# Ten mixing groups on one core: the step that follows each group is taken at a higher rate, and the first scores of the next attention are ordered differently

## The chip, the cores and the metric

The kernel runs on one core of one Trainium2 chip. The metric is the device time of one execution in microseconds, and lower is better. The core has a matrix engine (TensorE, PE in the rows; its weight loads are PEld), a vector engine (VectorE, DVE), an activation engine (ScalarE, ACT), GpSimd (POOL), and SyncE (SP), which issues nearly all transfers of this kernel, in its own order.

## The reference

Three layers follow each other on 8 batches of 576 tokens, 512 wide (8 heads of 64).

```
p_packed = sm_attn(p, k, v)              # 32 packed rows per head look at the 576 tokens
out      = sm_attn(q, p_packed, p_packed)# 576 tokens look at the 32 packed rows
x        = heads put side by side
u        = x + real(fft2(x))             # over tokens and channels of a batch
ch       = relu(norm(u) @ w_ch1) @ w_ch2 # 512 -> 2048 -> 512
y        = u + ch
logits   = y @ w_gate                    # 8 experts; a second gate decides per token whether
e        = argmax or the expert before   # it takes its own expert or that of the token before
out      = p[e] * (relu(y @ w1[e]) @ w2[e])
```

## The kernel before

Nearly every product is made of three fp16 products of high and low halves (`PASS`, line 162), so TensorE does most of the work and the other engines split, evict and normalize.

**Stages.** The attention and the transform of batch 0 come first. Then ten groups of the channel layer follow, in the order 0, 1, 2, R0, 3, 4, 5, 6, R1, 7 (line 1146). A numbered group is a batch's 512 tokens; R0 and R1 hold the 256 tokens of four batches that don't fill a tile. Behind them the experts' blocks run (`e1`, `e2`).

**A group** (`Mix`) has 16 first products `mm1(f)` (12 matmuls each, written `hp`) and 16 second products `mm2(f)` (12 matmuls each, 6 for R0 and R1, written `acc`), two steps apart. The last two second products of a group run between the first two first products of the next one. A numbered group so has 384 matmuls of its own.

**Beside it** run generators, which `tick` advances: the attention of the next batch at `ATT_RATE`, the splitting of the experts' weights at `EW_RATE`, and `after_mix` of the group before at `LAST_RATE`. A numbered group gives 2 ticks a step f, 28 from f = 2 to 15; R0 and R1 give 14. `after_mix` has four tiles (two for R0 and R1). For each it scales the tile into high and low halves (`xh`), transposes them by a transfer into the one buffer `xt`, stores them to `XS`, and later makes eight small matmuls `lp` (the logits) that VectorE evicts (`lsum`). It takes some 23 advances for four tiles. What isn't done when the next group begins is then taken at once (`drain`).

**Attention's steps around the change**, in their order: first scores (`scores`, line 361; per half of the heads, two tiles of 4 matmuls, written `s1`), their greatest, the exponentials, halves and a transposing transfer (`turn`: `ehl` to `et`), the product with v (`pps`, for which v is loaded and split, `vhl`), its transposition (`ptp`), and the second scores (`s2`, from q, loaded and split as `qh`, and `pth`). Then come the transform's products over channels (`gp`) and over tokens (`bp`, `zd`, `P`, `Q`, `X`).

**Buffers.** Attention and logits share two PSUM buffers (`psA`, tag `att`). k, v and q share two buffers (tag `qkv`): a half of v is loaded when the first scores have read that half of k, and a half of q when v is split.

**Order.** A scheduler takes the ready instruction of the smallest number, where numbers follow the program. `tc.high_priority(offset=SOON)` lowers an instruction's number by 200, so it may stand earlier than the code says. Each engine, SyncE too, then runs its own list in order. `scores` takes a PSUM buffer with its first matmul there.

Of the kernel before, what the change touches and what calls it, by code (L numbers as in the profile page):

```python
# [164 lines left out]
EW_RATE = 1.3  # L165
EWS = 2
CW0, CW1 = 5, 2
LAST_RATE = 1.2
R0_RATE = 1.6
R1_RATE = 1.2  # L170
AHEAD = 3
SOON = 200
# [7 lines left out]
def _build(tc, nc, ctx, A, stop):  # L180
# [132 lines left out]
    def attention(b):  # L313
        count = [0]

        def att(nm):
            count[0] += 1
            if b == 0 and count[0] % 3:
                return psO.tile([128, 512], F32, tag="o", name=nm)
            return psA.tile([128, 512], F32, tag="att", name=nm)  # L320
# [26 lines left out]
        pt = ap.tile([128, 4, 32], F32, tag="pt", name=f"p{b}")  # L347
# [3 lines left out]
        kts, vts, q32, qts = [], [], [], []  # L351
# [7 lines left out]
        s1, mxs, e32s = {}, {}, {}  # L359

        def scores(hf):
            s1[hf] = [att(f"s1_{b}_{hf}_{i}") for i in range(2)]

            for i in range(2):
                for p2 in range(2):
                    for r in range(2):
                        d, row = slice(64 * r, 64 * r + 64), 64 * p2 + 32 * r
                        nc.tensor.matmul(s1[hf][i][row:row + 32, :288], pt[d, 2 * hf + p2],  # L368
                                         kts[hf][d, p2, 288 * i:288 * i + 288], start=True, stop=True)
            (load_v if b else load_q)(hf)  # L370

        def greatest(hf):
# [21 lines left out]
        for steps in (((scores, 0),), ((greatest, 0),), ((exps, 0), (scores, 1)), ((turn, 0), (greatest, 1)),  # L394
                      ((exps, 1),), ((turn, 1),)):
            for fn, hf in steps:
                with tc.high_priority(offset=SOON if fn in (scores, greatest, exps) else 0):
                    fn(hf)
            yield
        rs = ap.tile([128, 2], F32, tag="rs", name=f"rs{b}")  # L400
# [8 lines left out]
        for hf in range(2):  # L409
# [13 lines left out]
            n = 0  # L423
# [133 lines left out]
        for k, (cs, hf) in enumerate(((0, 0), (0, 1), (1, 0), (1, 1))):  # L557
# [3 lines left out]
            for i in range(2):  # L561
                for n, (x, y) in enumerate(PASS):
                    nc.tensor.matmul(bp[:, :w], aeo[i][:, x, cs, cols], cst[:, 4 * i + 2 * cs + y, :w],  # L563
                                     start=i + n == 0, stop=False)
# [7 lines left out]
            if k == 2:  # L572

                zd = att(f"zd{b}")
                n = 0
# [460 lines left out]
    for n, _ in enumerate(attention(0)):  # L1036
        if n == CW0:
            while wdone[0] < CW1:
                next(cw)
            nc.sync.dma_start(cdt, A["cdt"])  # L1040
            nc.sync.dma_start(c3, A["c3"])
            nc.sync.dma_start(cst, A["cst"])
        if n == 30:
            wgf = wp.tile([128, 4, 9], F32, name="wgf")
            nc.sync.dma_start(wgf, A["wg"])
            nc.sync.dma_start(c16, A["c16"])
            nc.sync.dma_start(i32r, A["i32r"])
            nc.sync.dma_start(i32v, A["i32v"])
            nc.sync.dma_start(c32, A["c32"])
            split(wgh[:, :, 0], wgh[:, :, 1], wgf, 64.0)  # L1050
# [95 lines left out]
    for b in [0, 1, 2, "R0", 3, 4, 5, 6, "R1", 7]:  # L1146
# [11 lines left out]
        if prev is not None:  # L1158
            if last is not None:
                drain(last)  # L1160
            last = after_mix(prev.tiles)
            bg.append([last, 0.0, LAST_RATE])
        if not isinstance(b, str):
            if b + 1 < NB:
                ga = attention(b + 1)
                bg.append([ga, 0.0, ATT_RATE])
            if b == 1:
                bg.append([ew, 0.0, EW_RATE])
            if b == 7:
                actx.close()  # L1170
                open_moe()
                drain(ew)
                drain(last)
                r0 = routing(0)
                bg.append([r0, 0.0, R0_RATE])
# [69 lines left out]
```

## Time and profile before

| | |
|---|---|
| median of 3 runs (lowest, highest) | 1516.62 us (1511.03, 1521.59) |
| profiled execution, its own time | 1514.66 us |
| span in its trace | 1512.9 us |
| granted TensorE clock, mean | 0.971 |
| TensorE busy | 1403.3 us (93% of the span) |
| VectorE busy | 769.0 us (51%) |
| ScalarE busy | 460.5 us (30%) |

The page's busy times count instructions, not progress: the end of a matmul is modelled. Its slices show TensorE at nine tenths or more from the second tenth of the span on, and the granted clock at full speed nearly throughout. A row of the waits names the engine and line that waited and whom for; the time is idle time of that engine just before the instruction.

### The profile page before, as it was taken

To read this page: it belongs to the slowest core of one execution; us is meant where nothing else is said; L and a number is where in the kernel's file an instruction comes from. 1 tells how busy PE (TensorE), PEld (TensorE's weight loads), DVE (VectorE), ACT (ScalarE), POOL (GpSimd) and SP (SyncE) were. 2 spreads that over 40 slices of the span, in tenths; PEclk is the share of its full clock that TensorE was granted. 3 is DMA by queue.
4 is the path that set the end of the run, shared out by engine and by line. 5 is a ranking of instruction groups with operands and counts; after the bars stand their busy time and mean duration, and the time that the engine had idled before them with its cause. 6 is when DMAs were issued, how large, how long until landed. Compare 5 with 4: busy or idle time off the path is not lost. (4 is left out here: it accounts for less than half of the span.)

```text
span 1512.9 us, 28826 instructions
## 1 busy us (share of the span) xinstructions
PE 1403.3 (93%) x11340; PEld 825.5 (55%) x11340; DVE 769.0 (51%) x1615; ACT 460.5 (30%) x858; POOL 278.9 (18%) x296
## 2 busy tenths in 40 slices
PE   4588888998999899999999999999899999999996
PEld 3334434544564454454444456455677677777764
DVE  5789977567655766666766665433531111111110
ACT  3343444344333434434435333111111111111111
POOL 1312113203200420320321220000212121121211
PEclk6689999999999999999999999999999999999998
DMA  8275476386476637647656546244946636783371
GB/s 268 61 226 177 142 190 156 111 208 164 122 166 158 191 108 201 170 118 219 149 131 198 125 124 170 56 180 139 252 114 197 170 89 172 226 245 81 79 230 54
DMA packets 233163, 239.70 MB, mean 158 GB/s; under 512 B 168191, under 2 KB 179583, under 8 KB 232384
## 3 DMA queue, kind: packets, MB, share of 16 engines
q1 hardware_dynamic: 226464, 217.62, 52.6%
q0 software_dynamic: 6560, 20.19, 4.1%
q8 instruction: 91, 1.49, 0.4%
q14 instruction: 48, 0.39, 0.1%
HBM read 267.38 MB, written 53.74 MB: 212 GB/s over the span
## 5 line engine op out<-in xcount | busy, mean ns | idle before, releaser
L759 PE MATMUL acc<-w2h,ht 128*128 128x512 f16 x1728 | 410.3, 379 | 0.8 <-DVE ul L767 0.8
L739 PE MATMUL hp<-ut,w1h 128*128 128x512 f16 x1536 | 371.3, 383 | 5.9 <-DMA ut<-unh 5.2
L739 PEld LDWEIGHTS <-w1h 128*128 128x128 f16 x1920 | 183.7, 98 | 187.8 <-issue 21.0
L759 PEld LDWEIGHTS <-ht 128*128 128x128 f16 x1728 | 165.7, 98 | 185.2 <-issue 6.6
L1107 PE MATMUL ehp<-xgt,w1b 128*128 128x128 f16 x3936 | 232.6, 219 | 3.3 <-DMA w1b<-WS 2.2
L1107 PEld LDWEIGHTS <-w1b 128*128 128x128 f16 x3936 | 225.2, 98 | 15.5 <-DMA w1b<-WS 2.6
L1115 DVE SCALAR_TENSOR_TENSOR hx<-ehp,hx 128x512 f16<-128x512 f32 x82 | 56.6, 691 | 339.3 <-ACT hx L1114 335.5
L1125 PE MATMUL eo<-w2b,hx 128*128 128x512 f16 x984 | 219.2, 379 | 0.0
L747 DVE SCALAR_TENSOR_TENSOR ht<-hp,ht 128x512 f16<-128x512 f32 (+1 forms) x160 | 101.3, 633 | 165.9 <-ACT ht L746 165.7
L1125 PEld LDWEIGHTS <-hx 128*128 128x128 f16 x984 | 94.3, 98 | 106.3
L261 ACT ACTIVATE so<-se 128x512 f16<-128x512 f32 x128 | 79.8, 628 | 194.6 <-DMA WS<-so 154.6
L746 ACT ACTIVATE ht<-hp 128x512 f16<-128x512 f32 (+1 forms) x160 | 87.2, 546 | 138.6 <-PE hp L739 133.5
L1114 ACT ACTIVATE hx<-ehp 128x512 f16<-128x512 f32 x82 | 48.9, 597 | 185.9 <-PE ehp L1107 185.9
L262 DVE SCALAR_TENSOR_TENSOR so<-se,so 128x512 f16<-128x512 f32 x128 | 98.2, 776 | 10.7 <-ACT so L261 10.7
L1133 POOL DMA_INDIRECT out<-ys,sidx x41 | 41.5, 1013 | 332.2 <-ACT ys L1132 310.8
L1132 ACT ACTIVATE ys<-eo,scl 128x512 f32<-128x512 f32 x41 | 28.2, 687 | 179.2 <-PE eo L1125 179.2
L344 POOL TENSOR_TENSOR qh<-q,qh 128x1420 f16<-128x1420 f32 x12 | 34.6, 2880 | 257.3 <-ACT qh L343 233.9
L1075 POOL DMA_INDIRECT xg<-XS,gidx x41 | 42.2, 1029 | 174.9 <-DVE sidx L1031 103.9
L368 PE MATMUL s<-k,p 64*32 64x288 f32 x256 | 24.3, 478 | 24.8 <-DVE ru L648 11.6
L739 PE MATMUL hp<-utr,w1h 128*128 128x256 f16 x384 | 47.1, 272 | 0.0
L563 PE MATMUL bp<-cst,eh 128*128 128x289 f16 (+1 forms) x192 | 33.5, 317 | 13.2 <-ACT eh L540 6.5
L694 POOL TENSOR_TENSOR unh<-un,unh 128x512 f16<-128x512 f32 x32 | 38.6, 1216 | 30.7 <-ACT unh L693 30.7
(288 smaller groups left out, 1346.4 us busy)
## 6 DMA issues: line engine op xcount, KB each, us to landing
w1b<-WS SPq DMA_DIRECT2D x156, 512.0 KB
w2b<-WS SPq DMA_DIRECT2D x156, 512.0 KB
se<-in_w SPq DMA_DIRECT2D x64, 512.0 KB
WS<-so SPq DMA_DIRECT2D x128, 256.0 KB
sw<-in_wc SPq DMA_DIRECT2D x32, 512.0 KB
q<-in_qd SPq DMA_DIRECT2D x16, 710.0 KB
v<-in_vd SPq DMA_DIRECT2D x16, 640.0 KB
k<-in_kd SPq DMA_DIRECT2D x16, 576.0 KB
```

The source lines that it names most:

```text
L261: nc.scalar.activation(dst_hi, src, AF.Copy, scale=scale)
L262: nc.vector.scalar_tensor_tensor(dst_lo, src, scale, dst_hi, ALU.mult, ALU.subtract)
L739: nc.tensor.matmul(hp[:, :ntok], w1h[:, f, c, x], ut[:, 4 * y + c, :ntok], start=n == 0, stop=n == 11)
L746: nc.scalar.activation(ht[:, 0, :ntok], hp[:, :ntok], AF.Relu)
L747: pace[0] = nc.vector.scalar_tensor_tensor(ht[:, 1, :ntok], hp[:, :ntok], 0.0, ht[:, 0, :ntok], ALU.max, ALU.subtract).ins
L759: nc.tensor.matmul(self.acc[j], ht[:, x, 128 * j:128 * j + 128], w2h[:, f, y], start=f == 0 and n == 0, stop=f == 15 and n == 2)
L1075: nc.gpsimd.indirect_dma_start(out=g_, out_offset=None, in_=XS[0:rows], in_offset=bass.IndirectOffsetOnAxis(ap=gidx[:, b:b + 1], axis=0), ...
L1107: nc.tensor.matmul(hp[:, cols], w1b[b % RB][:, 2 * c + fg, x, cols], xt[b][:, 4 * y + c], start=n == 0, stop=n == 11, skip_group_check=True)
L1114: nc.scalar.activation(ht[:, fg, 0], hp, AF.Relu)
L1115: nc.vector.scalar_tensor_tensor(ht[:, fg, 1], hp, 0.0, ht[:, fg, 0], ALU.max, ALU.subtract)
L1125: nc.tensor.matmul(op, h[:, f // 4, x, 128 * (f % 4):128 * (f % 4) + 128], w2b[b % RB][:, f, y], start=n == 0, stop=n == 23)
L1133: nc.gpsimd.indirect_dma_start(out=A["out"], out_offset=bass.IndirectOffsetOnAxis(ap=sidx[:, b:b + 1], axis=0), in_=ys, in_offset=None, bo ...
```

## The change

`LAST_RATE` goes from 1.2 to 3, so four tiles of `after_mix` are through after some 8 of a numbered group's 28 ticks. In `scores` the first of the eight matmuls of a half keeps the place that the program gives it, and the other seven are lowered by 200; they are written so that the two halves of the tokens still follow each other. The loads behind them (v, or q for batch 0) are no longer lowered.

```diff
-LAST_RATE = 1.2
+LAST_RATE = 3
...
-            for i in range(2):
-                for p2 in range(2):
-                    for r in range(2):
-                        d, row = slice(64 * r, 64 * r + 64), 64 * p2 + 32 * r
-                        nc.tensor.matmul(s1[hf][i][row:row + 32, :288], pt[d, 2 * hf + p2],
-                                         kts[hf][d, p2, 288 * i:288 * i + 288], start=True, stop=True)
+            for n in range(8):
+                i, p2, r = n // 4, n // 2 % 2, n % 2
+                d, row = slice(64 * r, 64 * r + 64), 64 * p2 + 32 * r
+                with tc.high_priority(offset=SOON if n else 0):
+                    nc.tensor.matmul(s1[hf][i][row:row + 32, :288], pt[d, 2 * hf + p2],
+                                     kts[hf][d, p2, 288 * i:288 * i + 288], start=True, stop=True)
             (load_v if b else load_q)(hf)
...
-                with tc.high_priority(offset=SOON if fn in (scores, greatest, exps) else 0):
+                with tc.high_priority(offset=SOON if fn in (greatest, exps) else 0):
```

On TensorE before, around the end of group 3 (`hp12`) and in group 4 (`hp18`), beside which the attention of batch 5 runs (`s1_5`, `pps5`):

```order
L368 MATMUL s1_5_0_0_5882<-k5_0_5878,p5_5875 32x288 x4
L739 LDWEIGHTS w1h_127
L739 MATMUL hp12_15_5768<-ut3_4017,w1h_127 128x512
...
L368 MATMUL s1_5_0_1_5883<-k5_0_5878,p5_5875 32x288 x4
...
L368 MATMUL s1_5_1_0_5927<-k5_1_5880,p5_5875 32x288 x4
L368 MATMUL s1_5_1_1_5928<-k5_1_5880,p5_5875 32x288 x4
...
L759 MATMUL acc21_5915<-w2h_128,ht18_1_5848 128x512
L427 LDWEIGHTS et5_0_5949
L427 MATMUL pps5_6004<-vhl5_0_6005,et5_0_5949 64x128
```

The same place now:

```order
L739 MATMUL hp18_2_5867<-ut4_5528,w1h_127 128x512
L368 MATMUL s1_5_0_0_5886<-k5_0_5882,p5_5879 32x288 x2
L368 MATMUL s1_5_0_1_5887<-k5_0_5882,p5_5879 32x288
...
L759 MATMUL acc19_5919<-w2h_128,ht18_0_5820 128x512
L368 MATMUL s1_5_1_0_5937<-k5_1_5884,p5_5879 32x288 x2
...
L776 LDWEIGHTS xt12_5910
L776 MATMUL lp12_5982<-wgh_110,xt12_5910 128x18
...
L776 LDWEIGHTS xt13_5997
L776 MATMUL lp13_6049<-wgh_110,xt13_5997 128x18
L427 LDWEIGHTS et5_0_5959
L427 MATMUL pps5_6030<-vhl5_0_6031,et5_0_5959 64x128
```

The first scores moved from 24 group matmuls ahead of group 4's first (120 ahead of `pps5`) to 54 behind it (43 ahead of `pps5`); `pps5` itself moved by one, and nothing behind its second half moved but the logits. Two of the four logits now stand between scores and `pps5`; the other two follow it at 20 and 44 matmuls. It is the same in groups 2, 5 and 6, and nearly so in group 1, where the scores stood 93 matmuls ahead of `pps` and now stand 43 ahead. Beside group 3 they moved by 6 matmuls only (48 ahead of `pps` before, 42 now): the short R0 group lies ahead of it, and the attention of batch 4 starts inside group 3 in both versions.

SyncE's list before, at the same place:

```order
L329 DMA v5_0_5892<-in_vd 128x5x256
L329 DMA v5_1_5937<-in_vd 128x5x256
L391 DMA_TRANSPOSE et5_0_5949<-ehl5_0_5945 128x10x128
L309 DMA WS2_126<-so3_7_0_5788 128x1024
L309 DMA WS2_126<-so3_7_1_5801 128x1024
L334 DMA q5_0_6015<-in_qd 128x1420
L391 DMA_TRANSPOSE et5_1_5982<-ehl5_1_5978 128x10x128
L300 DMA se4_1_6064<-in_w1 128x1024
L348 DMA p6_7051<-in_pd 128x128
L334 DMA q5_1_6078<-in_qd 128x1420
L798 DMA_TRANSPOSE xt12_5975<-xh12_5942 128x8x128
```

And now:

```order
L329 DMA v5_0_5896<-in_vd 128x5x256
L798 DMA_TRANSPOSE xt12_5910<-xh12_5901 128x8x128
L799 DMA XS_124<-xh12_5901 128x1024
L329 DMA v5_1_5947<-in_vd 128x5x256
L799 DMA XS_124<-xh13_5952 128x1024
L391 DMA_TRANSPOSE et5_0_5959<-ehl5_0_5955 128x10x128
L798 DMA_TRANSPOSE xt13_5997<-xh13_5952 128x8x128
L309 DMA WS1_125<-so4_0_0_5973 128x1024
L391 DMA_TRANSPOSE et5_1_6004<-ehl5_1_6000 128x10x128
L334 DMA q5_0_6040<-in_qd 128x1420
...
L334 DMA q5_1_6122<-in_qd 128x1420
```

Transposes and stores of the halves (`xt`, `XS`) now stand between the loads of v, `et` and q, where they stood behind them.

## Rows read from the trace of the kernel before

**Rows 1.** Page, part 1: span, and busy time, share and instructions of each engine.

```profile
span 1512.9 us, 28826 instructions
PE 1403.3 (93%) x11340; PEld 825.5 (55%) x11340; DVE 769.0 (51%) x1615; ACT 460.5 (30%) x858; POOL 278.9 (18%) x296
```

**Rows 2.** Windows of groups 1 to 6: length, busy of each engine, PEclk, DMA share, GB/s.

```profile
196.50:304.00 107.50, 96.69 (x669) 48.81 (x665) 73.58 (x140) 42.59 (x81) 24.03 (x24) 1.00 0.60 156
304.00:416.00 112.00, 106.36 (x712) 52.35 (x713) 74.65 (x149) 44.56 (x85) 24.55 (x23) 0.98 0.63 164
...
464.00:571.00 107.00, 98.92 (x682) 49.77 (x680) 67.33 (x132) 43.07 (x82) 23.43 (x24) 0.98 0.57 157
571.00:682.00 111.00, 106.81 (x712) 52.62 (x712) 72.37 (x149) 44.69 (x84) 24.90 (x24) 0.97 0.59 160
682.00:792.00 110.00, 103.95 (x712) 51.91 (x712) 73.71 (x148) 44.73 (x84) 25.01 (x24) 1.00 0.62 164
792.00:903.00 111.00, 107.18 (x718) 53.08 (x719) 71.53 (x149) 45.48 (x85) 24.77 (x22) 0.98 0.54 152
```

**Rows 3.** Waits of TensorE, whole span: us in total, times, longest.

```profile
PE s L368 <- DVE ru L648: 11.6, 2, 9.5
PE lp L776 <- DVE g L474: 8.0, 5, 2.0
PE s L368 <- issue: 7.1, 3, 2.6
PE bp L563 <- DVE g L474: 4.3, 5, 1.2
PE pps L427 <- DVE vhl L416: 2.4, 3, 1.3
PE gp L469 <- DVE lsum L780: 2.0, 2, 1.1
```

**Rows 4.** Timeline: first scores after batch 0, and those beside group 4.

```profile
81.50 1.44 PE L739 MATMUL hp<-ut,w1h 128*128 128x512 f16 x3 [3.65 <-DMA ut<-unh]
...
571.78 0.69 PE L368 MATMUL s<-k,p 64*32 64x288 f32 x8 [2.58 <-issue]
...
574.60 2.66 PE L739 MATMUL hp<-ut,w1h 128*128 128x512 f16 x7
```

**Rows 5.** Timeline of group 4: a logits wait and what ScalarE did ahead of it.

```profile
635.22 0.63 ACT L525 ACTIVATE ah<-ee 32x512 f16<-32x512 f32 x1 [3.21 <-DVE ee L518]
...
637.64 0.17 PE L776 MATMUL lp<-wgh,xt 128*128 128x18 f16 x1 [2.01 <-DVE g L474]
```

**Rows 6.** Timeline of group 3, from the first scores to the second.

```profile
473.05 0.69 PE L368 MATMUL s<-k,p 64*32 64x288 f32 x8
...
481.10 2.75 PE L739 MATMUL hp<-ut,w1h 128*128 128x512 f16 x12
...
483.69 2.75 PE L759 MATMUL acc<-w2h,ht 128*128 128x512 f16 x12
...
487.35 1.03 PE L427 MATMUL pps<-vhl,et 128*64 128x128 f16 x30 [0.91 <-DMA et<-ehl]
...
491.24 0.33 SPq L334 DMA_DIRECT2D q<-in_qd  x1
...
498.79 1.37 ACT L343 CAST qh<-q 128x1420 f16<-128x1420 f32 x1
...
504.92 0.21 PE L491 MATMUL s<-pth,qh 128*128 128x64 f16 x1 [2.64 <-ACT pth L448]
```

**Rows 7.** Timeline: a logits transposition and the logits behind it, in two other stages.

```profile
968.99 1.24 SPq L798 DMA_TRANSPOSE xt<-xh  x1
...
972.10 0.18 PE L776 MATMUL lp<-wgh,xt 128*128 128x18 f16 x1 [0.32 <-DMA xt<-xh]
...
1059.13 1.24 SPq L798 DMA_TRANSPOSE xt<-xh  x1
...
1064.16 0.18 PE L776 MATMUL lp<-wgh,xt 128*128 128x18 f16 x1 [0.50 <-DMA xt<-xh]
```

## The prediction

> **What bounds the kernel now.** I read the page first. TensorE is busy for 1403.3 of 1512.9 us [rows 1], so the kernel is a chain of TensorE's instructions with some 110 us of holes, and only holes can be won. The clock is read with them, because a hole can leave the engine at the lower of its two levels for a while. The change touches groups 1 to 6, so the windows of those come next [rows 2]. Length less TensorE's busy time is 10.8, 5.6, 8.1, 4.2, 6.1 and 3.8 us: 38.6 us in six groups, of which group 3 (8.1) has the fewest matmuls displaced. Everything that the change can win lies in the other five, 30.5 us, and in the granted clock: 0.97 or 0.98 in four of the six windows. VectorE and ScalarE have room (some 70 and 44 us of 110), so a new wait would be one of order and latency, not of throughput. The list of TensorE's waits then says which instruction stood at a hole and whom it waited for [rows 3], and the timelines show single holes [rows 4 to 7].
>
> **What is removed: holes at the first scores.** In the old order they stand at the end of the group before, right behind the last transform products, and take the two PSUM buffers that those still hold. The holes sum to 7.1 us in three places ("issue"), and 2.1 in a fourth (11.6 less the longest, 9.5) [rows 3]: groups 2, 4, 5 and 6. Now the scores stand 78 group matmuls later. Twelve take 2.59 us (481.10 to 483.69) [rows 6], so one takes 0.216 and 78 take 16.8 us: the buffers are free by then. What is next in order is a group product that waits for nothing, so all of it is won: **-9.2**. The fifth hole, 9.5 us after batch 0, stays: right behind it the first group product waits 3.65 us more, for the transposed input of group 0 [rows 4], which the scores don't delay.
>
> **What is removed: holes in the middle of a group.** Logits waited 8.0 us in five places for the eviction of a channel product, the token products behind them 4.3 in five, and channel products 2.0 for the eviction of logits [rows 3]. The logits are gone from there. The last part is won (2.0). The first isn't: the buffer comes back no earlier, since ScalarE sat 3.21 us on VectorE's division before it came to the channel product [rows 5], and the first token product takes the logits' place in the wait, three group matmuls later. That wins 0.65 each, 3.2 in all. The token products' own waits (4.3) go, as they get a buffer that is one turn older. Together **-9.5**, between 5.2 (only the two sure parts) and 14.3 (all of it).
>
> The Trainium skill, "Perfetto Trace Analysis", Optimization Strategy, says that one gap repeating on the engine that should be saturated can mean too little SBUF or PSUM for the next tile. By that rule a user taken off the two buffers ends the whole hole, -14.3 and not -9.5; the row on ScalarE is why I take the smaller.
>
> **What comes with the holes: the clock.** Behind the hole at 571.78 seven group matmuls took 2.66 us [rows 4], where 7 times 0.216 is 1.5: 1.1 us lost beyond the hole. A mean of 0.97 over 111 us [rows 2] is 3.3 us short of full speed. If half of such losses in groups 2, 4 and 6 go with the holes, that is **-2** (0 to 5).
>
> **What is added: a short chain.** The work is the same; what moves is its place. `pps` and the second scores keep theirs, while the first scores, on which both hang by way of the exponentials, `et`, v and q, come 78 matmuls nearer. Group 3 already has such a spacing and is the measured price [rows 6].
> - *Product with v.* In group 3 the scores begin at 473.05 and `pps` at 487.35, after a wait of 0.91 for `et`: the chain takes 14.3 us. Now 43 group matmuls (9.3), both halves of the scores (some 2.5, at 0.69 for eight rows) and two logits (0.4) lie between: 12.2, so 2.1 us are missing. Part is paid at the logits ahead (next item); I take 1.5. At best 0, if those logits wait anyway; at worst 4.2, double the shortage, since four tiles of halves now share VectorE, ScalarE and SyncE with the chain, not two.
> - *Second logits.* They follow the first at 17 group matmuls, 3.7 us, with one `xt` buffer between them. From issue of the transposition to the logits it takes 3.1 us in a quiet stretch (968.99 to 972.10) and 5.0 in a busy one (1059.13 to 1064.16) [rows 7], and the issue comes behind the logits before. So 0 to 1.7 is missing. I take 0.8. The other two have over 5 us and are free.
> - *Second scores.* In group 3 they wait 2.64 us for ScalarE's copy of the transposed product [rows 6], which stands behind the split of q; q took 7.55 us from issue to that split (491.24 to 498.79). The spacing from first to second scores falls from 105 to 99 group matmuls, 1.3 us more. From 0.91 + 2.64 + 1.3 = 4.9 missing, 2.3 are paid in the two items above. 2.6 are left; I take 2.0, because there q's first half is issued a little earlier against v. Between 0 (another cause in group 3) and 5 (nothing paid ahead).
>
> That is 4.3 per group, in groups 1, 2, 4, 5 and 6: **+21.5**, where 0 to 11 per group are possible at the extremes. Their present waits of `pps` are in it and are taken off, about 2.0 of the 2.4 for v [rows 3]: **-2.0**. R0, R1 and group 7 have no attention beside them, so their logits move at no price; the group matmuls cover them, as they do now. What that costs if the cover is gone is the item on second logits, once for each.
>
> The Trainium skill, "Advanced Engine Details and Errata", X-Bar Transpose (TRN2), expects 350 to 400 GB/s from such a transposition, about 0.7 us for these 256 KB as an estimate. By that figure the second logits would never wait and the sum would be 4 us lower; the rows [rows 7] show four to seven times as long from issue to use, so they decide.
>
> **The sum.** -9.2 - 9.5 - 2 + 21.5 - 2.0 = -1.2 us. The profiled execution took 1514.66 us, span and what lies around it, so 1513.5 by its own time. It stood 2.0 under the median of the runs shown. Against that median the forecast is **1515 us**: no change.
>
> **Rivals.**
> - *The chain has room (faster).* Group 3 might be a bad model: it starts behind a short group, and its waits may come from there. For it: before, the five others show next to no wait at the second scores. Against it: there the scores are 120 matmuls ahead, so they can't show one. Then only the second logits cost, 5 times 0.8: 22.7 less 4.0, -18.7, or **1498 us**. With the whole of the 14.3 it is 1493. Chance 0.20.
> - *v and q arrive late (slower).* The place is SyncE's list: q's load waits until v is split, v's until the scores are read, and four transpositions and stores of halves now stand between them. All that was spread over the group now falls in the stretch between scores and second scores, with four tiles of halves where group 3 has two. The second scores don't move. So each microsecond by which q takes longer than the 7.55 [rows 6] is a hole in five groups. It decides from some 3.3 us on (16 us in all); with 4.5 it is 22 us over the forecast, **1537 us**, and the clock may add a few. For it: the chain in group 3 ends in just this wait. Against it: the transfer engines are only 0.54 to 0.63 busy in these windows [rows 2]. Chance 0.20.
> - *The change does nothing.* The orders show the moves, so this is no case of its own; that gains and new holes cancel is the forecast, chance 0.60.
>
> A measurement of this kernel tells about 1% from no change, here 15 us. The forecast case runs from 1502 to 1531 by the bounds of its terms; with parts of the two rivals the range is **1495 to 1538**. Faster by over 1%: 0.20; within 1%: 0.60; slower by over 1%: 0.20.
>
> **What would show it.** In the profile after, the holes at the first scores of groups 2, 4, 5 and 6 are gone, and the 9.5 us after batch 0 is still there. No logits wait on channel products; the token products wait about 1.4 us once in a group. New holes stand at the second logits (on `xt`), at `pps` (on `et`) and at the second scores (on the copy `pth` or on the split of q), some 4 us a group. If these are absent it is the first rival; if the second scores wait over 5 us in each of the five, the second. I am wrong in kind if a group product itself begins to wait, for its input `ht` or for a PSUM buffer of its own, because ScalarE or VectorE is held up by the halves.

## The result and the profile after

The change made the kernel slower: 1536.34 us median of four runs (1533.28 to 1538.49) against 1514.63, a ratio of 1.0144 with a 95% interval of 1.0114 to 1.0174. The forecast was 1515. The profiled execution took 1538.49 us. One execution each of two kernels below (e6_mid and e9_before_ew) took 1829 and 1828 us at a granted clock of 0.74 and is left out of their medians.

Page of the kernel after, part 1, which answers to [rows 1]:

```profile
span 1536.7 us, 28809 instructions
PE 1411.4 (92%) x11340; PEld 831.4 (54%) x11340; DVE 771.0 (50%) x1615; ACT 459.3 (30%) x858; POOL 280.3 (18%) x296
```

The same 11340 matmuls take 8.1 us more, and TensorE's idle time, span less busy, goes from 109.6 to 125.3 us. So two thirds of the 23.8 us by which the traced span is longer are holes. The rest, 8.1 us, goes with a lower granted clock (0.965 over the span, 0.971 before).

TensorE's waits after (line, whom for, us in total, times, longest), which answer to [rows 3]:

```profile
PE lp L776 <- DMA xt<-xh: 23.2, 17, 3.6
PE pps L427 <- DMA et<-ehl: 12.3, 3, 9.6
PE gp L469 <- DVE ee L500: 10.7, 6, 2.8
PE s L368 <- DVE ru L648: 9.3, 1, 9.3
PE bp L563 <- DVE g L474: 7.0, 6, 2.0
...
PE bp L563 <- DVE big L567: 6.0, 4, 1.9
...
PE lp L776 <- DVE ht L747: 2.4, 1, 2.4
...
PE hp L739 <- DVE ht L747: 0.3, 1, 0.3
```

What was to go is gone: of the first scores' holes only the 9.3 us after batch 0 are left, and no logits wait for channel products. But the logits now wait 23.2 us in 17 places for their transposition, and the token products `bp` wait 13.0 us for `g` and `big`. Before, the logits' wait was 4.0 us in four places, and that for `big` was 0.3 ([rows 3] have 4.3 for `g`):

```profile
PE lp L776 <- DMA xt<-xh: 4.0, 4, 2.4
...
PE bp L563 <- DVE big L567: 0.3, 1, 0.3
```

There is no wait for `pth` or for q's split at the second scores, and `pps` waits for `et` as before (12.1 us in three then). The next windows are cut at the same matmuls of both kernels, some way ahead of each group's first product (19.5 us for R1), and the short one ends inside R1 (length, then busy us and instructions of TensorE, its weight loads, VectorE, ScalarE and GpSimd, then PEclk, DMA share, GB/s): those of groups 2 and 4 and the one that ends in R1, first after, then before.

```profile
320.70:435.10 114.40, 103.21 (x713) 52.17 (x712) 75.91 (x154) 44.96 (x86) 26.72 (x26) 1.00 0.61 158
...
568.20:682.60 114.40, 105.58 (x714) 52.85 (x713) 73.22 (x147) 45.09 (x85) 25.10 (x24) 0.99 0.57 158
...
906.00:949.70 43.70, 40.14 (x245) 23.28 (x244) 28.89 (x77) 13.54 (x27) 7.10 (x7) 0.96 0.53 143
```

```profile
317.90:424.20 106.30, 101.51 (x681) 51.86 (x680) 71.03 (x140) 40.79 (x75) 26.38 (x26) 0.98 0.60 157
...
557.10:668.70 111.60, 106.88 (x714) 52.66 (x713) 71.77 (x147) 45.22 (x85) 24.91 (x24) 0.97 0.60 163
...
886.90:925.70 38.80, 37.97 (x229) 22.29 (x228) 26.55 (x72) 11.16 (x23) 7.09 (x7) 1.00 0.49 129
```

The windows of groups 2 and 4 stand 11.2 and 8.8 us idle, where they stood 4.8 and 4.7. R1 has no attention beside it, and its window is 4.9 us longer all the same; 2.9 of that is one wait of logits.

One group's chain of logits, from the timeline after beside group 4 (start, duration, engine, line, [idle before <- whom for]):

```profile
602.82 0.74 DVE L791 SCALAR_TENSOR_TENSOR xh<-uu,rsc,xh 128x512 f16<-128x512 f32 x1
...
604.33 1.89 SPq L391 DMA_TRANSPOSE et<-ehl  x1
...
605.13 0.17 PE L776 MATMUL lp<-wgh,xt 128*128 128x18 f16 x1
...
606.34 2.17 SPq L798 DMA_TRANSPOSE xt<-xh  x1
...
610.85 0.18 PE L776 MATMUL lp<-wgh,xt 128*128 128x18 f16 x1 [1.69 <-DMA xt<-xh]
...
611.25 0.18 DVE L780 TENSOR_REDUCE lsum<-lp 128x9 f32<-128x18 f32 x1 [1.93 <-PE lp L778]
...
611.41 0.73 DVE L791 SCALAR_TENSOR_TENSOR xh<-ul,rsc,xh 128x512 f16<-128x512 f32 x1
...
612.34 1.55 SPq L798 DMA_TRANSPOSE xt<-xh  x1
...
616.42 1.37 ACT L343 CAST qh<-q 128x1420 f16<-128x1420 f32 x1 [1.91 <-DMA q<-in_qd]
617.70 0.59 ACT L746 ACTIVATE ht<-hp 128x512 f16<-128x512 f32 x1
...
619.03 0.10 PEld L776 LDWEIGHTS <-xt 128*128 128x128 f16 x1 [2.93 <-DMA xt<-xh]
619.03 0.18 PE L776 MATMUL lp<-wgh,xt 128*128 128x18 f16 x1 [2.44 <-DVE ht L747]
```

It closes on itself. The second tile's halves are ready at 603.56, and the logits at 605.13 free the one `xt`, but the issue of `et` holds SyncE until 606.22. The transposition is issued at 606.34, and 4.51 us later the next logits start, late by 1.69. In groups 1, 2, 5 and 6 too the second transposition goes 0.10 to 0.12 us behind the issue of the first `et`, with its halves ready for 2.6 to 3.4 us. In group 4 VectorE's list then has the sums of the late logits ahead of the third tile's halves, so it too stands 1.93 us; those halves end at 612.14, their transposition goes at 612.34, and its logits start 6.69 us later, late by 2.44. The row names `ht`, but the weight load of the same logits waited for `xt`. This part of the loop, by way of VectorE, stands in group 4 alone: in the other four groups the third tile's halves are ready 2.5 to 4.0 us before their transposition, which goes 0.17 or 0.18 us behind the issue of the second `et`. Over the whole trace a transposition comes 3.1 to 8.5 us ahead of its logits, median 4.8 over the first 26 of 36, while the order leaves 17 to 24 group matmuls, 3.7 to 5.2 us.

### The profile page after: what moved, and what is told of

Same layout as the page of the kernel before. It is cut to its first block, busy times and chain, and to the rows that moved or that the text cites. A ratio compares the mean times of both kernels' runs of the same rounds, so it can differ in the third digit from the quotient of the medians.

```text
span 1536.7 us, 28809 instructions
## 1 busy us (share of the span) xinstructions
PE 1411.4 (92%) x11340; PEld 831.4 (54%) x11340; DVE 771.0 (50%) x1615; ACT 459.3 (30%) x858; POOL 280.3 (18%) x296
## 5 line engine op out<-in xcount | busy, mean ns | idle before, releaser
L759 PE MATMUL acc<-w2h,ht 128*128 128x512 f16 x1728 | 417.0, 383 | 0.7 <-DVE ul L767 0.7
L739 PE MATMUL hp<-ut,w1h 128*128 128x512 f16 x1536 | 376.2, 386 | 6.8 <-DMA ut<-unh 5.6
L739 PEld LDWEIGHTS <-w1h 128*128 128x128 f16 x1920 | 186.8, 99 | 191.8 <-issue 24.0
L747 DVE SCALAR_TENSOR_TENSOR ht<-hp,ht 128x512 f16<-128x512 f32 (+1 forms) x160 | 101.7, 635 | 190.7 <-ACT ht L746 190.1
L262 DVE SCALAR_TENSOR_TENSOR so<-se,so 128x512 f16<-128x512 f32 x128 | 109.3, 859 | 17.2 <-ACT so L261 17.2
L563 PE MATMUL bp<-cst,eh 128*128 128x289 f16 (+1 forms) x192 | 32.4, 309 | 21.1 <-DVE g L474 7.0
L563 PEld LDWEIGHTS <-eh 128*128 128x128 f16 x192 | 19.6, 104 | 36.9 <-issue 14.9
```

The costliest lines, as they stand in the source:

```text
L262: nc.vector.scalar_tensor_tensor(dst_lo, src, scale, dst_hi, ALU.mult, ALU.subtract)
L739: nc.tensor.matmul(hp[:, :ntok], w1h[:, f, c, x], ut[:, 4 * y + c, :ntok], start=n == 0, stop=n == 11)
L747: pace[0] = nc.vector.scalar_tensor_tensor(ht[:, 1, :ntok], hp[:, :ntok], 0.0, ht[:, 0, :ntok], ALU.max, ALU.subtract).ins
L759: nc.tensor.matmul(self.acc[j], ht[:, x, 128 * j:128 * j + 128], w2h[:, f, y], start=f == 0 and n == 0, stop=f == 15 and n == 2)
```

## The experiments

All times are medians; ratios with their 95% intervals are against the kernel before, run beside each on the same chip, and the sets of runs come from different chips. Wherever `xt` has two buffers, two scratch tiles (`t16`, `beq`) share or lose one to make room. "Logits' wait" is TensorE's wait at `lp` for `xt`, from each one's list of waits.

| kernel | rate | first scores | experts' weights | us | ratio, 95% | logits' wait |
|---|---|---|---|---|---|---|
| before | 1.2 | old | early | 1511.6 to 1514.6 | 1 | 4.0 |
| after | 3 | new | early | 1536.3 | 1.0144 (1.0114 to 1.0174) | 23.2 |
| e1_rate | 3 | old | early | 1517.0 | 1.0017 (0.9997 to 1.0037) | 19.5 |
| e2_scores | 1.2 | new | early | 1514.8 | 1.0011 (0.9989 to 1.0033) | 4.7 |
| e3_xt2 (two `xt`) | 3 | new | early | 1526.2 | 1.0074 (1.0041 to 1.0107) | 22.8 |
| e4_before_xt2 (two `xt`) | 1.2 | old | early | 1512.1 | 0.9999 (0.9974 to 1.0025) | 3.5 |
| e5_delay | 3, 12 us later | new | early | 1524.6 | 1.0080 (1.0049 to 1.0111) | 22.4 |
| e6_mid | 3 | half way | early | 1547.1 | 1.0186 (1.0115 to 1.0257) | 42.8 |
| e7_ew | 3 | new | late | 1518.8 | 1.0038 (1.0009 to 1.0066) | 19.3 |
| e8_xs (store by GpSimd) | 3 | new | early | 1541.9 | 1.0180 (1.0127 to 1.0233) | 35.9 |
| e9_before_ew | 1.2 | old | late | 1512.4 | 0.9983 (0.9965 to 1.0001) | 2.9 |
| e10_ew_xt2 (two `xt`) | 3 | new | late | 1513.0 | 0.9984 (0.9963 to 1.0004) | 13.4 |
| e11_scores_ew | 1.2 | new | late | 1504.6 | 0.9919 (0.9884 to 0.9954) | 3.0 |
| e12_rate_ew | 3 | old | late | 1530.3 | 1.0088 (1.0057 to 1.0119) | 24.1 |
| f2_two_ahead | 3, logits a tile later | new | early | 1514.0 | 1.0019 (0.9997 to 1.0041) | 3.5 |
| f3_two_ahead_ew | 3, logits a tile later | new | late | 1498.1 | 0.9909 (0.9877 to 0.9940) | 3.0 |
| f4_rate2 | 2 | new | early | 1509.7 | 0.9984 (0.9965 to 1.0002) | 7.1 |
| f5_rate2_ew | 2 | new | late | 1513.6 | 1.0010 (0.9986 to 1.0033) | 3.9 |
| f6_old_scores_ew | 3, logits a tile later | old | late | 1500.3 | 0.9924 (0.9897 to 0.9952) | 3.3 |
| f7_old_scores | 3, logits a tile later | old | early | 1501.0 | 0.9918 (0.9891 to 0.9946) | 3.0 |

Single executions of one kernel lie up to 12 us either side of its median (before: 1504 to 1524), and so do the profiled ones.

**First: which half of the change, and is it the one buffer?** Edits: `LAST_RATE = 3` alone in the kernel before; the scores' order alone; and `xt` with `bufs=2` in the changed kernel and in the kernel before.

e1_rate: 

> The kernel before with the rate alone (3 for 1.2); the first scores keep their old places. Theory A (the loss comes from the logits, which now stand 17 to 24 group matmuls apart while their one buffer is refilled by a transposition of 3 to 5 us): 1530 to 1545 us, logits waiting for the transposition 18 to 28 us in all (4.0 before), and the holes ahead of the first scores still there. Theory B (the loss comes from the later first scores, which push the attention chain back): 1510 to 1520 us, with the waits of the gate products for the exponentials near the 4.6 us of before.

e2_scores: 

> The kernel before with the first scores' new order alone; the rate stays 1.2, so the logits keep their old distance of 48 to 60 group matmuls. Theory A: 1503 to 1516 us, the holes ahead of the first scores of groups 2 to 6 gone, the logits' wait for the transposition near 4 us. Theory B: 1528 to 1540 us, with 8 to 12 us of gate products waiting for the exponentials and the products behind them late.

e3_xt2: 

> The changed kernel with two buffers for the transposed halves instead of one (the room comes from one routing scratch and one attention scratch tile that share or lose a buffer). Theory A: the next transposition no longer waits for the logits ahead of it; logits' waits for transpositions fall from 23.2 to under 8 us and the time to 1510 to 1522 us. Theory B: the waits at the logits go, but the time stays at 1532 to 1540 us, since the same time is waited later in the chain. A third case: the waits at the logits stay above 15 us, since what is late is the halves themselves (VectorE, ScalarE) or SyncE's list and not the buffer.

e4_before_xt2: 

> The kernel before with the same two buffers, as a control: both theories 1510 to 1519 us, since its logits wait 4.0 us in all for transpositions; a value outside says that the buffers' room, and not the wait, moves the time.

Each half alone is 2 to 4 us slower, which the intervals don't tell from nothing. Theory B fell with e2, and theory A missed e1 by 13 us although the wait that it named is there (19.5). In e3 the third case came: 10 us better, and the logits wait as long. A second buffer lets a transposition start earlier, but its logits still follow at nearly the same distance (median 5.3 us against 4.8 over the first 26). Which wait gave the 10 us stays open. The control is even. e2 also shows where the first scores' gain goes: the second scores, TensorE's waits of that kernel.

```profile
PE pps L427 <- DMA et<-ehl: 15.7, 6, 9.6
PE s L491 <- DVE pth L449: 11.1, 6, 3.0
```

**Second: do the two halves collide, and where?** The edits to the changed kernel:

```
e5  bg.append([last, 0.0, LAST_RATE])  ->  bg.append([last, -12.0, LAST_RATE])
e6  high_priority(offset=SOON if n else 0)  ->  offset=SOON if n else 50
e7  EW_RATE = 1.3, EWS = 2  ->  EW_RATE = 2.0, EWS = 7
e8  nc.sync.dma_start(XS[...], hl)  ->  nc.gpsimd.dma_start(XS[...], hl)
```

e5_delay: 

> The changed kernel, but what follows a group begins 48 group matmuls (about 12 us) later, at the same rate of 3: logits at 72 to 135 matmuls behind the last sums of the group instead of 24 to 87. Neither half of the change cost time alone, so theory C: the loss is their meeting; with the later first scores the exponentials' transposes, V's load and split and Q's loads fall into the same 15 us as the halves, transposes and copies of the finished group, on ScalarE's, VectorE's and SyncE's lists. It expects 1508 to 1520 us here. Theory A (logits 17 to 24 matmuls apart with one transposed buffer) expects 1528 to 1540 us, since that distance is unchanged.

e6_mid: 

> The changed kernel with the first scores about half way back (43 and 35 group matmuls earlier for the two halves, some 9 us; of 78 in the change). Theory C: most of the loss goes, 1513 to 1524 us. If the later place of the scores costs nothing by itself and the logits alone cost (theory A): 1530 to 1540 us.

e7_ew: 

> The changed kernel with the preparation of the expert weights kept out of the first 7 of a group's 16 slices (2 before), and its rate raised from 1.3 to 2.0 for the rest. Theory D: ScalarE stands still behind the stores of these weights in the very stretch in which both chains need it, so the time falls to 1515 to 1526 us. Theory C with the two chains alone: 1530 to 1540 us.

e8_xs: 

> The changed kernel with the halves' copy to memory (36 of 256 KB) issued from GpSimd's queue instead of SyncE's, which took 0.4 to 1.0 us of SyncE each between two transposes. Theory E: SyncE's one list in the first third is what is short; 1515 to 1527 us. Theory C with ScalarE and VectorE as the place of the meeting: 1531 to 1541 us.

e6 went against both theories: nearer to the old place, it is no faster than the change, and its logits wait 42.8 us. Its timeline shows how (beside group 4):

```profile
606.45 0.75 DVE L389 TENSOR_TENSOR ehl<-e,ehl 128x576 f16<-128x576 f32 x1
607.27 1.38 ACT L343 CAST qh<-q 128x1420 f16<-128x1420 f32 x1 [2.50 <-DMA q<-in_qd]
607.28 1.36 SPq L391 DMA_TRANSPOSE et<-ehl  x1
...
608.72 2.88 POOL L344 TENSOR_TENSOR qh<-q,qh 128x1420 f16<-128x1420 f32 x1 [26.52 <-ACT qh L343]
609.04 0.71 ACT L790 ACTIVATE xh<-ul,rsc 128x512 f16<-128x512 f32 x1
...
609.78 2.37 DVE L791 SCALAR_TENSOR_TENSOR xh<-ul,rsc,xh 128x512 f16<-128x512 f32 x1
...
612.38 1.23 SPq L798 DMA_TRANSPOSE xt<-xh  x1
...
617.58 0.20 PE L776 MATMUL lp<-wgh,xt 128*128 128x18 f16 x1 [5.91 <-DMA xt<-xh]
```

SyncE's list now has both `et` ahead of the first `xt`, but the halves themselves are late. ScalarE waits 2.50 us for q and splits it first, so its part of the halves comes at 609.04. VectorE's part then takes 2.37 us (0.74 for the next tile) while GpSimd splits q, and ends at 612.15. The transposition goes 0.23 later, 5.20 us before its logits, which stand 5.91 us. It is the same in all of groups 1 to 6: VectorE's part takes 2.36 or 2.37 us, the transposition goes 0.02 to 0.23 us behind it, and the six waits at the first logits are 32.4 of the 42.8 us.

In e8 some 0.4 to 1.0 us of SyncE's issue less per tile brought no gain (1541.9 against 1536.3), and theory E fell. The Trainium skill, "DMA: Bandwidth & Descriptors", Rules for kernel authors, says that spreading transfers over several issuing engines only saves issue time; here that saving brought nothing. e5 got half of the way, where theory C expected most of it: the window that ends in R1 is back at 38.8 us. There only the first tile of a group stands far ahead of its logits (10 to 19 us); the later ones stand 4 to 8 us, and the logits wait as long as before. (That trace is of an execution at 1515.9 us, 8.6 under the median.) e7 won 17.6 us, as theory D said.

**Third: is it the experts' weights?** The edit of e7 in the kernel before (e9), with the rate alone (e12), with the scores alone (e11) and with two `xt` (e10).

e9_before_ew: 

> The kernel before with the expert weights' preparation kept out of the first 7 slices of a group (rate 2.0 for 1.3), the control for the same edit on the changed kernel, which it brought from 1536 to 1519 us. Theory D (the loss of the change needs the expert weights as third party in the first third): 1508 to 1518 us, no gain, since with the logits spread wide nothing is short there. Rival F (the edit gains by itself, whatever the order around it): 1490 to 1502 us.

e12_rate_ew: 

> The rate of 3 alone (first scores in their old places) with the late expert weights. Theory D: 1508 to 1519 us, like the rate alone (1517) less a few us of ScalarE's and SyncE's waits. Rival F: 1495 to 1503 us.

e11_scores_ew: 

> The first scores' new order alone (rate 1.2) with the late expert weights. In the first-scores kernel the 9.5 us won at the first scores went to 8.5 us more at the second scores (pth) and 3.6 us at the token products (et), which stand behind the same lists; if the expert weights on those lists are the cause, these shrink and it takes 1502 to 1511 us, below the kernel before; if the two chains' own length is (30 matmuls from scores to products), 1512 to 1518 us.

e10_ew_xt2: 

> The changed kernel with both cures together: late expert weights and two transposed buffers (1519 and 1526 us one by one, from 1536). If each takes away a wait of its own in SyncE's list: 1505 to 1513 us. If both only remove the same wait: 1515 to 1522 us.

Theory D fell with e12: the rate alone is slow even with the weights out of the way. With e1, e7, after and e12 the rate now costs 4, 14, 22 and 18 us, while the scores cost 2 or win 8 at the old rate. e11 beats the kernel before by 0.8%. e10, at 1513.0, lies at the upper edge of the case in which each cure takes away a wait of its own. What the kernels at 1517 us and more share is a logits' wait of 19 us and more; no other has over 13.4.

**Fourth: the distance itself.** f2 moves the logits (and has two `xt`, since two tiles are held at once). Halves and transposes nearly stay where the change put them: the order has them two advances later, and beside group 4 the first three transposes come 6.3, 11.3 and 17.7 us behind the start of the group's sums (6.3, 11.8 and 17.8 in the changed kernel). f3 adds e7's edit; f4 and f5 are the changed kernel and e7 at a rate of 2.

```diff
-            if j:
-                yield
-                logits(tiles[j - 1][1])
-                yield
-            xt = wp.tile(..., bufs=1)
+            yield
+            if j > 1:
+                logits(tiles[j - 2][1])
+            yield
+            xt = xts[col] = wp.tile(..., bufs=2)
...
-        for _ in range(4):
-            yield
-        logits(tiles[-1][1])
+        for t in tiles[-2:]:
+            for _ in range(4):
+                yield
+            logits(t[1])
```

f2_two_ahead: 

> The changed kernel (rate 3, later first scores) with two transposed buffers and each tile's logits taken one tile later, so that some 36 to 45 group matmuls (8 to 10 us) lie between a transposition and its logits instead of 17 to 24; halves and transposes stay in the first third. Over the kernels run so far the time goes with the logits' wait for transpositions: 2.9 to 4.7 us in all at 1505 to 1515 us (five kernels), 13 to 43 us at 1513 to 1547 us (nine). Theory A' (that short distance is the cost, whatever crowds SyncE's list) expects waits of under 6 us and 1508 to 1520 us. Theory G (halves and transposes packed in the first third cost by crowding VectorE, ScalarE and SyncE, wherever the logits stand) expects 1528 to 1538 us, with the time waited at the gate products instead.

f3_two_ahead_ew: 

> The same with the late expert weights (rate 2.0 after slice 7). Theory A': like the first-scores kernel with late expert weights (1504.6) or below, since the rate then costs nothing: 1498 to 1508 us. Theory G: 1512 to 1522 us, like the changed kernel with late expert weights (1519).

f4_rate2: 

> The changed kernel at a rate of 2 instead of 3: logits 30 to 36 matmuls apart (6.5 to 8 us) with one buffer. Theory A': the distance now covers a transposition's 3 to 5 us and the halves' 2 us, so the waits fall to 4 to 10 us and the time to 1512 to 1522 us. Theory G: about half of the loss stays, 1522 to 1530 us.

f5_rate2_ew: 

> The same rate of 2 with the late expert weights. Theory A': 1500 to 1508 us, at or below the 1504.6 of rate 1.2. Theory G: 1509 to 1516 us, half way between the 1504.6 of rate 1.2 and the 1518.8 of rate 3.

f2 takes 22.3 us off the changed kernel and f3 20.7 off e7: theory A' in both. f4, which widens the distance by the rate and keeps one buffer, takes off 26.6, 2 us better than A' said. f5 misses A' by 6 us and lies where theory G put it. Its logits wait only 3.9, but its profile has a wait of 13.5 us of `pps` for v's split that f4 doesn't have. Why late weights bring that at this rate alone stays open. TensorE's waits of f2 show what the logits' waits had covered:

```profile
PE pps L427 <- DMA et<-ehl: 15.8, 7, 9.6
...
PE s L491 <- DVE pth L449: 4.7, 4, 1.6
PE gp L469 <- DVE ee L500: 4.5, 4, 2.3
...
PE lp L777 <- DMA xt<-xh: 3.5, 4, 2.2
...
PE ptp L442 <- DVE ppr L437: 3.2, 3, 2.0
PE s L491 <- POOL qh L344: 2.8, 3, 1.1
PE s L491 <- DVE lsum L781: 2.6, 4, 0.8
```

(L777 is L776 of the others.) The second scores wait 10.1 us in all. In f3 they don't wait; this is its page and, in the second fence, its waits at the first scores and logits:

```profile
span 1492.7 us, 28823 instructions
PE 1394.4 (93%) x11340; PEld 824.6 (55%) x11340; DVE 757.8 (51%) x1615; ACT 459.7 (31%) x858; POOL 274.9 (18%) x296
```

```profile
PE s L368 <- DVE ru L648: 9.3, 1, 9.3
...
PE lp L777 <- DMA xt<-xh: 3.0, 3, 2.0
```

**Fifth: the first scores without the logits' wait.** f2 and f3 with the first scores in their old places.

f6_old_scores_ew: 

> The best version so far (rate 3, logits one tile later, late expert weights; 1498) with the first scores put back to their old places. With the logits out of the way, Theory A' gives the first scores' order what it won with late expert weights at a rate of 1.2 (1512.7 to 1504.6): 1504 to 1511 us here, and 7 to 10 us of holes at the first scores are back. Rival H (the order of the first scores is worth nothing once the logits stand far enough): 1495 to 1502 us.

f7_old_scores: 

> The changed kernel with the logits one tile later (1514) and the first scores in their old places, expert weights as in the kernel before. The rate's own gain (8 us of waits of the logits for the channel products) without its price: Theory A' 1504 to 1512 us, since at early expert weights the first scores' order won nothing (1512.5 to 1514.8 at a rate of 1.2). If the rate still costs by crowding the first third (theory G): 1514 to 1522 us.

f6 says H: with late weights the new order is worth 2.2 us (1500.3 to 1498.1), which is within the noise. f7 is against G and comes out 3 us better than A' said: the rate wins when its logits stand far enough, and with early weights the new order then costs 13.0 us (1501.0 to 1514.0). TensorE's waits in f7, where the first scores' holes are back, the second scores hardly wait, and the token products wait as in the changed kernel:

```profile
PE s L368 <- DVE ru L648: 14.2, 3, 9.5
PE pps L427 <- DMA et<-ehl: 11.2, 2, 9.6
PE bp L563 <- DVE g L474: 6.9, 7, 1.7
PE bp L563 <- DVE big L567: 6.4, 5, 2.1
...
PE s L368 <- issue: 4.2, 2, 2.4
...
PE s L491 <- DVE pth L449: 1.5, 1, 1.5
```

Four pairs of kernels now differ in the logits' distance (and the second buffer) alone. Moving them away wins 16.0 us from e1 to f7, 22.3 from the change to f2, 20.7 from e7 to f3 and 30.0 from e12 to f6; between chips the kernel before differs by 3 us. The second buffer alone won 10.2 (e3) and 5.8 (e10), so 12.2 and 14.9 are left for the distance where both were run.

f3 is the fastest version found: 0.9909 of the kernel before (0.9877 to 0.9940), and 38 us under the change. f6 and f7 are not told from it by their intervals.

## Why the prediction was wrong

The change comes apart along before, f7, f2, after: 1512.9 - 11.9 (the rate, with its logits far) + 13.0 (the first scores' order) + 22.3 (the logits near, with one buffer) = 1536.3. These medians come from different chips; by the ratios the three terms are 12, 15 and 19 us.

- **The step that failed is the item "Second logits"**: 0.8 us a group, 4 in all, where moving the logits away again is worth 22.3. In the trace after, the second logits of the five groups wait 10.9 us. Its sentence "The other two have over 5 us and are free" is wrong: they wait 7.5. So is "R0, R1 and group 7 have no attention beside them, so their logits move at no price": those beside R1 wait 2.9 and those beside R0 1.2. I compared two transpositions of other stages (3.1 and 5.0 us) with the spacing that the order gives, and left out the rest of the loop: logits free the buffer, SyncE takes what stands ahead in its list, and in group 4 VectorE makes the next halves only behind the late logits' sums. So a late tile can make the next one late.
- **Holes in the middle of a group**, -9.5 with some of the clock's -2: the size came out (f7 wins 11.9), the places did not. The logits' 8.0 and the channel products' 2.0 are gone, but the token products, which were to be left with 4.8 in place of 4.6, wait 13.3 in f7 and 13.0 after. These rows together win 1.3 us. f7's trace has 7.9 us less idle time than the kernel before and 5.9 less busy time for the same matmuls, so that the number fits is in good part luck.
- **Holes at the first scores**, -9.2: right as holes. 18.4 us at the first scores in f7 are 9.3 in f2.
- **Product with v and second scores**, 3.5 a group, 17.5: right in kind, though after shows neither. In f2 the second scores wait 10.1 us, 8.6 more than in f7, where 10 was forecast, and `pps` waits 4.6 more for `et` (15.8 for 11.2; 7.5 forecast). With the -9.2 and the -2.0 this part of the sum was +6.3 and measures +13.0; smaller waits at other products make up part of the rest. In the changed kernel the logits' waits come ahead of both places and cover them. I priced waits one by one as if each came on top; here the larger one hid the ones that I had forecast.
- What made the second scores late is not the chain alone: with late expert weights the same order waits nothing there (f3). I had not counted the splitting of those weights as a third user of VectorE, ScalarE and SyncE in the first third.
- **The rivals.** 1537 us was the second rival's number, but not its mechanism: no second scores waited. So the number is luck. My sign of being wrong in kind, group products waiting for `ht`, did not come: they wait 0.3 us in one place, and the 2.4 us row that names `ht` is at the logits.
- The sum's "1502 to 1531 by the bounds of its terms" is 1% either way; its bounds added up give 1486 to 1555.
- The 0.7 us for a transposition, worked out from the bandwidth that the Trainium skill expects ("Advanced Engine Details and Errata", X-Bar Transpose (TRN2)), was rightly set aside; my own 3.1 to 5.0 was still too short for the stretch in question, where 4.51 and 6.69 are shown.

Open: why the rate alone costs 4 us with early weights (e1) and 18 with late ones (e12) at not very different logits' waits (19.5 and 24.1), what the second buffer alone won in e3, why the token products wait longer at a rate of 3, and f5's wait for v's split.

## What to carry to other kernels

When a step that hangs on a transfer is taken at a higher rate, count the distance from the issue of the transfer to its first reader as it will be in the new order, with everything between, and move the reader a turn later before the rate is raised: with that, the same rate won 0.8% (f7), where it had won nothing (e1). The Trainium skill has it in short ("DMA: Bandwidth & Descriptors", Rules for kernel authors: issue early, wait late); f2 shows its worth here, 22.3 us against the changed kernel, of which 12.2 are against the same kernel with two buffers (e3). And take waits that a change adds in their order along the engine: the first large one hides the later ones, and removing it brings them out.

## What the runs showed of the hardware

- The issue of one transposition of 256 KB holds SyncE 1.24 us in a quiet stretch ([rows 7]) and up to 3.44 us in the changed kernel, there in group 2; from issue to reader it takes 3.1 to 8.5 us.
- A tile of weights' halves on VectorE (`so`, L262), 0.68 us elsewhere, took 2.37 us at 618.93 of the changed kernel, while GpSimd's split of q ran from 617.87 for 2.88 us. In the traces before, after and e6_mid the single rows of VectorE that take over 1 us more than the median of their kind are 10, 12 and 11. All of them run while GpSimd is at work, and none reads PSUM. `ht` (L747), which does, keeps its 0.69 us beside the same split. No run takes the two engines apart.
